# Partial sums of a second matrix product held in DRAM by adding DMAs, and a filter spectrum copied once and duplicated by DMA

## Chip, cores and metric

The kernel runs on one core of a Trainium2 chip. The metric is the device time of one execution in microseconds. The core has five engines with an in-order queue each: TensorE (PE, with its weight loads shown as PEld), VectorE (DVE), ScalarE (ACT), GpSimd (POOL) and SyncE (SP, which only issues DMAs). ACT and POOL issue DMAs too.

## The reference

All arrays are float32; B = 1, S = 2048 rows, D = 576 channels, Dff = 4608.

```python
xn = layernorm(A_q)                                   # over the channels, no scale or shift
# A: two state-space convolutions and a gate
k_shift = causal conv of A_k with A_shift_k           # 4 taps for each channel
kv = k_shift * A_v
y = irfft(rfft(pad(kv)) * rfft(pad(A_ssm_k)))[:S] + kv * A_ssm_D
# B: two matrix products
h = relu(xn @ B_w1)                                   # 2048 x 576 by 576 x 4608
out = A_q + xn * y + h @ B_w2
```

## The kernel before

**Rows and batches.** The 2048 rows are 16 tiles `t` of 128 rows, four batches `b` of four tiles. Dff is cut into 18 pairs of 256. The rows go through in two halves of two batches; each half runs over all 18 pairs, so `n` counts 36 pairs, and with two batches each there are 72 visits `(n, s)` in the main loop at the end of the program.

**Two products.** A visit does the first product for 512 rows and 256 columns of h. From the third pair on, `quad` does it with a Strassen-like scheme in four parts: sums of pieces of x and of w1 are made beforehand, and VectorE adds the results in PSUM (`psa`, L574, and `psb`, L577). Every float32 operand is split in a high part, made by ScalarE, and a low part, made by VectorE (`ll`, L532) or, for the weights, by GpSimd (`split_lo`, L424). `unit` does the second product for one tile and one half of the 576 output channels: 12 matmuls of 288 columns (two pairs; 6 where there is one) into one of three PSUM banks, and then VectorE adds the bank to the SBUF tile `acc` (L610 for batch 0, which also scales by the rows' 1/std, and L614). The `acc` tiles begin as x, loaded by `load_acc`; those of the first half are stored to `fin` in DRAM when the half is done.

**The convolution** is a generator, `conv`, with four stages: **k** (first step of the filter's transform, L656 with `prepare` L690), **x** (the four taps, L742 to L751, and the first step of the signal's transform), a middle stage **m** (second step for both, product of the spectra, first step back, L824 to L883) and **o** (last step back, gate and sum, L886 to L976). In stage m each of 32 groups makes its spectrum of the filter (`k1`, `k2`, four half copies by ScalarE for each half of the channels, L845 to L848), then that of the signal, multiplies, and goes back one group later. In stage o, `gate` multiplies by x less its mean, `add` scales by 1/std and adds to `acc`, or for the first half to `ft`, read back from `fin`, which is then stored to `out`.

**What sets the order.** `tick`, called from the matmul loops with the number of columns done, advances a clock and draws the next piece of `conv` when the clock allows. The constants `W_FK`, `W_FX`, `W_FM`, `W_FO` are the costs of a piece of each stage, `SHARE` the part of the work by whose end the convolution is to be finished; `begin_stream` turns them into a rate. `here` puts a piece of the convolution behind the latest work of the products on VectorE and ScalarE (`done`). A scheduler then fixes each engine's order. SP issues nearly all loads and stores in its order.

Of the kernel before, what the change touches and what calls it, by code (L numbers as in the profile page):

```python
# [17 lines left out]
P = 128  # L18
# [31 lines left out]
SHARE = 0.96  # L50
# [3 lines left out]
W_FK, W_FX, W_FM, W_FO = 1.73, 3.5, 1.94, 2.2  # L54
# [6 lines left out]
SUMS = {"b11": 0, "t1": 1, "t2": 2, "t3": 3, "t4": 4}  # L61
# [44 lines left out]
def h3_ffn_kernel(ctx: ExitStack, tc, x, k, v, shift_k, ssm_k, ssm_D, w1, w2, fwd, inv, mid, out):  # L106
# [23 lines left out]
    fin = dram.tile([HT // 2, P, 2, D], F32, name="fin")  # L130
# [23 lines left out]
    def load_x(t, tag, bufs, **queues):  # L154
        pair = xp.tile([P, 2, D], F32, tag=tag, name=f"acc{t}", bufs=bufs)
        move(pair, x, slice(t, t + 2), **queues)
        return pair

    def load_acc(t, **queues):
        pairs[t] = load_x(t, f"acc{t // BT % HB}", BT // 2, **queues)  # L160
        acc[t], acc[t + 1] = pairs[t][:, 0, :], pairs[t][:, 1, :]
# [120 lines left out]
    def first_xT(srcs):  # L282
# [5 lines left out]
        neg = zp.tile([P, BT], F32, tag="neg", name="neg")  # L288
        behind = None
        for t in range(BT):  # L290
            if t % 2 == 0:
                pair = row_tiles(t)
            xn = pair[:, t % 2, :]
            if t % 2 == 0:
                with tc.issue_after(behind.ins) if behind else nullcontext():
                    stats(t, srcs[t])
                    behind = centred(xn, srcs[t], t)
            else:
                nc.scalar.activation(xn, srcs[t], AF.Copy, scale=-1.0 / D,
                                     accum_out=neg[:, t:t + 1])  # L300
                done["act"] = nc.scalar.activation(xn, srcs[t], AF.Identity,
                                                   bias=neg[:, t:t + 1])
# [11 lines left out]
        with tc.issue_after(done["dve"].ins):  # L314
            for t in range(1, BT, 2):
                stats(t, srcs[t])
            inv_std(0, BT)

    def second_xT(srcs):
# [7 lines left out]
        xn = []  # L327
        for t in range(BT, HT):
            if t % 2 == 0:
                pair = row_tiles(t)  # L330
            xn.append(pair[:, t % 2, :])
            normalized(xn[-1], srcs[t], t)
# [229 lines left out]
    def quad(n, s, m):  # L562
# [11 lines left out]
        nc.vector.tensor_tensor(pa[:, other], pb[:, first], m5, OP.add)  # L574
        yield
        run_seq(pb[:, first], product(n, s, "s3", "t3"))
        nc.vector.tensor_tensor(pb[:, other], pb[:, first], m5, OP.add)  # L577
# [9 lines left out]
    work = []  # L587

    def unit(ns, s, b, i, h, last):
# [15 lines left out]
        for i, (a, m) in enumerate(seq):  # L605
            nc.tensor.matmul(ps[:, :NH], a, m, start=i == 0, stop=i == len(seq) - 1)  # L606
            if i % 6 == 5:
                tick(6 * NH)
        if b == 0:
            done["acc"] = nc.vector.scalar_tensor_tensor(  # L610
# [544 lines left out]
```

## Time and profile before

| what | value |
|---|---|
| three runs | 1133.09, 1128.83, 1132.33 us; median 1132.33 |
| the profiled execution, its own time | 1130.09 us |
| its span in the profile | 1128.1 us |
| mean granted TensorE clock | 0.98 |
| HBM read and written | 122.12 MB and 43.25 MB |

The span is from the first to the last instruction of the profile; some 2 us lie around it. All rows and windows in this document are of profiled executions, and in us from the start of the span. In the windows of the prediction the stages of the convolution lie about so: the first pairs before it 0 to 140, loads of the filter 140 to 200, stage k 200 to 312, stage x 312 to 550, the change to the second half and the start of stage m 550 to 600, stage m to 950, stage o 950 to 1092, the last units to 1128.

### The profile page before, as it was taken

To read this page: it belongs to the slowest core of one execution; us is meant where nothing else is said; L and a number is where in the kernel's file an instruction comes from. 1 tells how busy PE (TensorE), PEld (TensorE's weight loads), DVE (VectorE), ACT (ScalarE), POOL (GpSimd) and SP (SyncE) were. 2 spreads that over 40 slices of the span, in tenths; PEclk is the share of its full clock that TensorE was granted. 3 is DMA by queue.
4 is the path that set the end of the run, shared out by engine and by line. 5 is a ranking of instruction groups with operands and counts; after the bars stand their busy time and mean duration, and the time that the engine had idled before them with its cause. 6 is when DMAs were issued, how large, how long until landed. Compare 5 with 4: busy or idle time off the path is not lost.

```text
span 1128.1 us, 21092 instructions
## 1 busy us (share of the span) xinstructions
PE 1067.1 (95%) x7761; PEld 1025.5 (91%) x7761; DVE 803.6 (71%) x1309; ACT 668.3 (59%) x1454; POOL 489.6 (43%) x492
## 2 busy tenths in 40 slices
PE   8979998999988798898999999999999999999998
PEld 5779998999988788898998999999999999999897
DVE  5578733677759999888466667676576665589985
ACT  4434422798824444443368878888887887465451
POOL 3243444455435444564433344433343443545541
PEclk9998998999998999998999999999999999999999
DMA  6035598355574554453894434442334432666654
GB/s 173 25 96 189 214 147 133 114 161 165 167 200 143 159 149 136 140 166 106 300 321 129 128 108 119 121 135 87 111 113 133 119 116 93 168 176 175 206 167 105
DMA packets 139154, 166.75 MB, mean 148 GB/s; under 512 B 47566, under 2 KB 99536, under 8 KB 138541
## 3 DMA queue, kind: packets, MB, share of 16 engines
q1 hardware_dynamic: 126156, 151.24, 46.7%
q0 software_dynamic: 12576, 13.44, 5.2%
q8 instruction: 61, 1.00, 0.4%
q10 hardware_dynamic: 320, 0.74, 0.3%
q14 instruction: 41, 0.33, 0.1%
HBM read 122.12 MB, written 43.25 MB: 147 GB/s over the span
## 4 chain that ended last, share of the span: by engine, by line
PE 67%; DVE 17%; DMA 5%; SPq 4%; issue 3%; ACT 3%; POOL 1%; POOLq 0%; DVEq 0%; ACTq 0%
PE pso L606 28%; PE psb L525 18%; PE psa L525 8%; PE psf L824 6%; DVE e L745 3%; SPq L679 3%; PE psh L525 2%; DVE c L746 2%; PE psf L656 2%; DMA r<-in_w 1%; DVE xs L650 1%; DVE ll L532 1%; DVE acc L614 1%; DVE acc L610 1%; DVE c L751 1%
## 5 line engine op out<-in xcount | busy, mean ns | idle before, releaser
L606 PE MATMUL pso<-w,hh 128*128 128x288 f32 x2304 | 469.9, 298 | 11.0 <-DVE acc L610 6.9
L606 PEld LDWEIGHTS pso<-w,hh 128*128 128x128 f32 x2304 | 371.6, 190 | 20.9 <-DVE acc L610 7.8
L424 POOL TENSOR_TENSOR g<-r,g 128x512 fp32r<-128x512 f32 (+2 forms) x178 | 207.4, 1174 | 379.2 <-ACT g L453 297.4
L606 PE MATMUL pso<-w,ll 128*128 128x288 f32 x1152 | 320.8, 297 | 3.9 <-DVE ll L532 3.9
L525 PE MATMUL psb<-t,g 128*128 128x256 f32 x1632 | 248.2, 287 | 26.2 <-DVE psa L574 14.1
L525 PEld LDWEIGHTS psb<-t,g 128*128 128x128 f32 x1632 | 220.3, 191 | 33.7 <-DVE psa L574 16.7
L606 PEld LDWEIGHTS pso<-w,ll 128*128 128x128 f32 x1152 | 211.3, 190 | 6.5 <-DVE ll L532 4.8
L424 POOL TENSOR_TENSOR w<-r,w 128x576 fp32r<-128x576 f32 x72 | 114.6, 1593 | 73.1 <-ACT w L511 72.9
L478 POOL TENSOR_TENSOR r<-r 128x256 f32<-128x256 f32 x136 | 115.6, 868 | 62.2 <-DMA r<-in_w 59.8
L614 DVE TENSOR_TENSOR acc<-pso,acc 128x288 f32<-128x288 f32 x224 | 96.7, 450 | 57.7 <-PE pso L606 56.9
L525 PE MATMUL psa<-b,g 128*128 128x256 f32 x816 | 122.1, 286 | 0.0
L531 ACT ACTIVATE hh<-psa 128x512 fp32r<-128x512 f32 x68 | 40.7, 598 | 127.2 <-PE psa L525 126.8
L525 PEld LDWEIGHTS psa<-b,g 128*128 128x128 f32 x816 | 109.8, 193 | 0.2
L453 ACT ACTIVATE g<-r 128x512 fp32r<-128x512 f32 (+2 forms) x178 | 91.2, 535 | 29.3 <-POOL r L478 12.1
L532 DVE SCALAR_TENSOR_TENSOR ll<-psa,hh 128x512 fp32r<-128x512 f32 x68 | 46.7, 686 | 39.7 <-ACT hh L531 39.5
L531 ACT ACTIVATE hh<-psb 128x512 fp32r<-128x512 f32 x68 | 40.7, 598 | 49.3 <-PE psb L525 46.5
L532 DVE SCALAR_TENSOR_TENSOR ll<-psb,hh 128x512 fp32r<-128x512 f32 x68 | 46.6, 686 | 29.1 <-ACT hh L531 28.7
L650 DVE TENSOR_TENSOR ks<-kt,ks 64x288 fp32r<-64x288 f32 x64 | 54.4, 849 | 17.3 <-ACT ks L649 15.7
L525 PE MATMUL psb<-b,g 128*128 128x256 f32 x408 | 62.1, 286 | 0.0
L860 DVE TENSOR_TENSOR k<-psf,k 128x288 f32<-128x288 f32 x64 | 28.8, 454 | 46.0 <-ACT sw L859 37.9
L525 PEld LDWEIGHTS psb<-b,g 128*128 128x128 f32 x408 | 55.1, 193 | 0.0
L610 DVE SCALAR_TENSOR_TENSOR acc<-pso,rstd,acc 128x288 f32<-128x288 f32 x80 | 39.4, 511 | 19.7 <-PE pso L606 19.1
(138 smaller groups left out, 1778.7 us busy)
## 6 DMA issues: line engine op xcount, KB each, us to landing
r<-in_w SPq DMA_DIRECT2D x72, 288.0 KB, 4.0
r<-in_w SPq DMA_DIRECT2D x35, 512.0 KB, 4.1
zk<-zk SPq DMA_DIRECT2D x32, 288.0 KB, 2.7
zx<-zx SPq DMA_DIRECT2D x32, 288.0 KB, 3.5
ztk<-zk SPq DMA_DIRECT2D x32, 288.0 KB, 3.1
ztx<-zx SPq DMA_DIRECT2D x32, 288.0 KB, 2.9
zy<-vo SPq DMA_DIRECT2D x32, 288.0 KB, 3.4
zo<-zy SPq DMA_DIRECT2D x32, 288.0 KB, 3.6
```

The costliest lines, as they stand in the source:

```text
L424: return nc.gpsimd.tensor_tensor(dst, src, hi, OP.subtract)
L453: nc.scalar.activation(hi, src, AF.Copy)
L478: nc.gpsimd.tensor_tensor(dst, a, b, op)
L525: nc.tensor.matmul(ps, a, m, start=start and i == 0, stop=i == len(seq) - 1, skip_group_check=not start)
L531: done["act"] = nc.scalar.activation(hh, ps, AF.Relu)
L532: lows.append(nc.vector.scalar_tensor_tensor(ll, ps, 0.0, hh, op0=OP.max, op1=OP.subtract))
L606: nc.tensor.matmul(ps[:, :NH], a, m, start=i == 0, stop=i == len(seq) - 1)
L610: done["acc"] = nc.vector.scalar_tensor_tensor(acc[t][:, dc], ps[:, :NH], rstd[:, t:t + 1], acc[t][:, dc], op0=OP.mult, op1=OP.add)
L614: done["acc"] = nc.vector.tensor_tensor(acc[t][:, dc], ps[:, :NH], acc[t][:, dc], OP.add)
L650: nc.vector.tensor_tensor(dst[other], src[own], dst[own], OP.subtract)
L679: nc.sync.dma_start(kt[halves(h)[0], d:d + KD, :], src)
L824: nc.tensor.matmul(ps[:, :NH], a, m[:, cols], start=n == 0, stop=n == 2)
```

## The change

**Sums of the second product.** `acc` no longer holds sums. A DRAM tile `total` is filled with x by eight DRAM-to-DRAM DMAs near the start. Each `unit` copies its PSUM bank (scaled for batch 0) to one half of a small tile `g`, four of which rotate; ScalarE copies before the convolution begins and in its stages x and o, VectorE in stages k and m. After two units one DMA issued by GpSimd adds the tile to `total`. The last units of the second half load `total` back in pairs of tiles (`load_total`), add PSUM to it on VectorE, and store each unit to `out`. The tiles of x at the start are normalised in place. `fin` is gone: `ft` is read from `total`, and for the second half stage o adds its result to `total` by a DMA.

**Filter's spectrum.** ScalarE copies each half of `k1` and `k2` once; a DMA on SP duplicates it to the other 64 partitions. The filter's part of a group is done one group before the signal's, with three buffers instead of two. The minus sign moves from `k2` to `sw`.

**Stage o.** The gate's normalisation of x becomes one ScalarE pass with scale and bias (`shift` is -mean/std), and VectorE multiplies and adds without scaling.

**Order.** The costs of the four stages, `SHARE` and some buffer counts change; `tick` can draw two pieces after a part of `quad`, and one in a unit, after its first 6 matmuls.

```diff
-SHARE = 0.96
+SHARE = 0.955
-W_FK, W_FX, W_FM, W_FO = 1.73, 3.5, 1.94, 2.2
+W_FK, W_FX, W_FM, W_FO = 1.875, 4.06, 1.77, 2.1
+BY_ACT = "zxo"
+G_BUFS = 4
...
-    fin = dram.tile([HT // 2, P, 2, D], F32, name="fin")
+    total = dram.tile([NB, P, BT, D], F32, name="total")
...
+    def load_total(t, h):
+        b, i = divmod(t, BT)
+        pair = xp.tile([P, 2, NH], F32, tag="g", name=f"last{t}_{h}", bufs=G_BUFS)
+        nc.sync.dma_start(pair, total[b, :, i:i + 2, h * NH:(h + 1) * NH])
+        for n in range(2):
+            acc[t + n, h] = pair[:, n]
...
-            if i % 6 == 5:
-                tick(6 * NH)
+            if c % 6 == 5:
+                tick(6 * NH, c == 5)
+        if final:
+            if h == 0 and i % 2 == 0:
+                for m in range(2):
+                    load_total(t, m)
+            to = acc[t, h]
+            done["acc"] = nc.vector.tensor_tensor(to, ps[:, :NH], to, OP.add)
+            for u, queue in ((0, nc.sync), (1, nc.scalar if t == T - 1 else nc.sync)):
+                queue.dma_start(out[u, :, t, dc], to[halves(u)[0]])
+            return
+        if i % 2 == 0:
+            g = xp.tile([P, 2, NH], F32, tag="g", name=f"sum{ns[0]}_{t}_{h}", bufs=G_BUFS)
+            parts_[0] = g
+        to, src = parts_[0][:, i % 2], ps[:, :NH]
+        act = stage[0] in BY_ACT
         if b == 0:
-            done["acc"] = nc.vector.scalar_tensor_tensor(
-                acc[t][:, dc], ps[:, :NH], rstd[:, t:t + 1], acc[t][:, dc],
-                op0=OP.mult, op1=OP.add)
+            if act:
+                done["act"] = nc.scalar.activation(to, src, AF.Copy, scale=rstd[:, t:t + 1])
+            else:
+                done["acc"] = nc.vector.tensor_scalar(to, src, rstd[:, t:t + 1], None,
+                                                      op0=OP.mult)
+        elif act:
+            done["act"] = nc.scalar.activation(to, src, AF.Copy)
         else:
-            done["acc"] = nc.vector.tensor_tensor(acc[t][:, dc], ps[:, :NH], acc[t][:, dc],
-                                                  OP.add)
+            done["acc"] = nc.vector.tensor_copy(to, src)
+        if i % 2:
+            nc.gpsimd.dma_start(total[b, :, i - 1:i + 1, dc], parts_[0], accum_op=OP.add)
...
                         ps, cols = run(*parts["k", g], 0, h)
                         nc.scalar.activation(k1[:64, cols], ps[:64], AF.Copy)
-                        nc.scalar.activation(k1[64:, cols], ps[:64], AF.Copy)
-                        nc.scalar.activation(k2[:64, cols], ps[64:], AF.Copy, scale=-1.0)
                         nc.scalar.activation(k2[64:, cols], ps[64:], AF.Copy)
+                        if h:
+                            nc.sync.dma_start(k1[64:], k1[:64])
+                            nc.sync.dma_start(k2[:64], k2[64:])
...
-                        nc.vector.scalar_tensor_tensor(ys[i], rest[i][1], mv[:, t, 0:1], ys[i],
-                                                       op0=OP.subtract, op1=OP.mult)
+                        q = rest[i][1]
+                        nc.scalar.activation(q, q, AF.Identity, scale=rstd[:, t:t + 1],
+                                             bias=shift[:, t:t + 1])
+                        nc.vector.tensor_tensor(ys[i], ys[i], q, OP.mult)
...
                     else:
+                        nc.gpsimd.dma_start(total[t // BT, :, t % BT, :], ys[i],
+                                            accum_op=OP.add)
                         added.add(t)
...
+    for b in range(NB):
+        for u in range(U):
+            nc.sync.dma_start(total[b, halves(u)[0]], x[u, :, b * BT:(b + 1) * BT, :])
```

What this does to the order on the engines is shown at three places. The first is VectorE in stage x. Before, about the eleventh pair (`pso_6_1` is the bank of tile 6, second half; `c` and `e` are the taps):

```order
L614 TENSOR_TENSOR acc_226<-pso_4_1_4410,acc_226 128x288
L745 TENSOR_TENSOR e_3_4156<-k_3460,sk 128x576
L577 TENSOR_TENSOR psb_0_4181<-psb_0_4181,m_11_0_4195 128x256
L746 TENSOR_TENSOR c_4102<-c_4102,e_3_4156 128x576
L614 TENSOR_TENSOR acc_226<-pso_5_1_4453,acc_226 128x288
L751 TENSOR_TENSOR c_4102<-c_4102,v_4049 128x576
L745 TENSOR_TENSOR e_1_4256<-k_4046,sk 128x576
L532 SCALAR_TENSOR_TENSOR ll_0_0_4296<-psa_0_4182,hh_0_0_4295 128x512
L614 TENSOR_TENSOR acc_229<-pso_6_1_4505,acc_229 128x288
```

and VectorE in the changed kernel, one pair later in the same stage:

```order
L578 TENSOR_TENSOR psa_0_4473<-psb_0_4472,m_12_0_4486 128x256
L760 TENSOR_TENSOR c_4531<-k_4442,sk 128x576
L763 TENSOR_TENSOR e_1_4541<-k_4285,sk 128x576
L764 TENSOR_TENSOR c_4531<-c_4531,e_1_4541 128x576
L581 TENSOR_TENSOR psb_0_4472<-psb_0_4472,m_12_0_4486 128x256
L763 TENSOR_TENSOR e_2_4583<-k_4146,sk 128x576
L764 TENSOR_TENSOR c_4531<-c_4531,e_2_4583 128x576
L536 SCALAR_TENSOR_TENSOR ll_0_0_4575<-psa_0_4473,hh_0_0_4574 128x512
```

The rows that empty a PSUM bank of the second product stand no longer between the taps; they are on ScalarE.

The second place is GpSimd in stage x, with the weights of the eleventh pair (`r_11`; `g` and `w` are split weights, `wx` constants of the transform). Before:

```order
L424 TENSOR_TENSOR g_0_3818<-r_11_3639,g_0_3818 128x512
L424 TENSOR_TENSOR w_10_1_3854<-r_10_1_3565,w_10_1_3854 128x576
L424 TENSOR_TENSOR g_1_3851<-r_11_3639,g_1_3851 128x512
L424 TENSOR_TENSOR g_2_3895<-r_11_3639,g_2_3895 128x512
L424 TENSOR_TENSOR g_3_3939<-r_11_3639,g_3_3939 128x256 x2
```

and GpSimd with the same weights in the changed kernel:

```order
L428 TENSOR_TENSOR g_0_3903<-r_11_3719,g_0_3903 128x512
L428 TENSOR_TENSOR w_10_1_3940<-r_10_1_3646,w_10_1_3940 128x576
L656 DMA wx_4081<-in_fwd 128x256
L639 DMA total<-sum_0_0_3922 128x2x288
L428 TENSOR_TENSOR g_1_3937<-r_11_3719,g_1_3937 128x512
L639 DMA total<-sum_2_0_4001 128x2x288
L428 TENSOR_TENSOR g_2_3982<-r_11_3719,g_2_3982 128x512
```

The adding DMAs, each of which waits for a copy on ScalarE, now stand between the splits of the weights.

The third place is SP at the end of the program. Before, only the outputs of the last tiles stand there:

```order
L150 DMA out<-acc_6989 64x1152 x2
L150 DMA out<-acc_6992 64x1152 x2
L150 DMA out<-acc_6740 64x1152 x2
L150 DMA out<-acc_6743 64x576 x2
L618 DMA out<-acc_6743 64x288 x2
```

and SP at the end of the changed kernel (`last_0` and `last_1` are the two halves of the channels; the last two of them are tiles 14 and 15):

```order
L621 DMA out<-last_0_14399 64x288 x2
L621 DMA out<-last_1_14401 64x288 x2
L621 DMA out<-last_0_14399 64x288 x2
L621 DMA out<-last_1_14401 64x288 x2
L167 DMA last_0_14443<-total 128x2x288
L167 DMA last_1_14445<-total 128x2x288
L621 DMA out<-last_0_14443 64x288 x2
```

The loads of the sums of tiles 14 and 15 stand behind the outputs of tiles 12 and 13. At the other end of SP's queue, the eight DMAs that fill `total` stand behind the loads of x for the second batch and ahead of the second pair's weights.

More of the change, by code (lines that the diff above doesn't have):

```diff
@@ L326, in second_xT @@
             inv_std(BT, BT)
[L327 to L332, printed above, removed]
+        xn = [srcs[t] for t in range(BT, HT)]
+        for i, row in enumerate(xn):
+            normalized(row, row, BT + i)
         for c in range(5):
@@ L664, in here @@
             yield
+    stage = ["z"]
+    shift = const.tile([P, T], F32, name="shift")
     def conv():
+        stage[0] = "k"
         with tc.tile_pool(name="fk", bufs=2) as fp:
@@ L1120, in h3_ffn_kernel @@
             phase([n], s, b, True)
-        if half == 1 and m == 0:
-            base = HT + (1 - second) * BT
-            for t in range(base, base + BT, 2):
-                load_acc(t)
     while work:
```

152 lines of the change are left out of this document (78 added, 74 removed).

## The prediction

> **What bounds the kernel now.** I read the page first, then the table of windows with one row per stage, then TensorE's waits inside the one stage that stands out, then VectorE's groups there.
>
> ```profile
> PE 1067.1 (95%) x7761; PEld 1025.5 (91%) x7761; DVE 803.6 (71%) x1309; ACT 668.3 (59%) x1454; POOL 489.6 (43%) x492
> ```
>
> TensorE is busy 95% of the span, so at first sight nothing but fewer matmuls could help, and the change removes none. The table by stage says more (columns: window, its length, then busy time and instruction count of PE, PEld, DVE, ACT, POOL, then clock, DMA share, GB/s).
>
> ```profile
> core 0: us, PE busy (x) PEld busy (x) DVE busy (x) ACT busy (x) POOL busy (x), PEclk, DMA share, GB/s
> 0.00:140.00 140.00, 125.13 (x779) 108.51 (x779) 97.58 (x201) 57.78 (x118) 51.55 (x54) 0.96 0.46 139
> 140.00:200.00 60.00, 55.20 (x399) 54.03 (x400) 19.66 (x37) 15.05 (x31) 25.90 (x29) 0.94 1.02 135
> 200.00:312.00 112.00, 110.05 (x830) 107.27 (x829) 84.06 (x125) 96.53 (x187) 58.12 (x69) 1.00 0.52 156
> 312.00:550.00 238.00, 211.10 (x1492) 201.06 (x1491) 202.67 (x278) 94.75 (x202) 114.57 (x112) 0.96 0.53 152
> 550.00:600.00 50.00, 50.00 (x384) 49.37 (x383) 29.29 (x54) 29.44 (x66) 20.47 (x21) 1.00 0.96 320
> 600.00:950.00 350.00, 347.64 (x2627) 341.77 (x2626) 234.75 (x385) 291.05 (x671) 142.08 (x126) 1.00 0.38 115
> 950.00:1092.00 142.00, 138.43 (x1046) 135.25 (x1045) 112.80 (x189) 74.94 (x162) 72.30 (x77) 1.00 0.63 179
> 1092.00:1128.00 36.00, 29.56 (x217) 28.27 (x215) 22.83 (x43) 8.76 (x20) 4.61 (x7) 0.96 0.40 104
> ```
>
> I take 550 to 600 as TensorE undisturbed: 384 matmuls in 50 us, 7.68 per us. From 140 us on, all stages hold the same mixture of 256- and 288-column matmuls, so a window's count over 7.68 is the time its work needs. Stage k (200 to 312) needs 108.1 of 112, **stage x (312 to 550) 194.3 of 238, a loss of 43.7 us**, 600 to 950 needs 342.1 of 350, stage o (950 to 1092) 136.2 of 142. In stage x VectorE was busy 202.67 us: more than the 194.3 TensorE needs. Elsewhere VectorE's share of the needed time is 0.78 (k), 0.69 (600 to 950), 0.83 (o). So stage x is bound by VectorE; TensorE bounds the rest but for the two ends. What TensorE waited for in stage x agrees (columns: waiter, releaser, us in total, times, longest):
>
> ```profile
> PE psb L525 <- DVE psa L574: 12.6, 6, 4.5
> PE pso L606 <- DVE acc L610: 5.2, 2, 4.1
> PE pso L606 <- DVE ll L532: 3.4, 3, 1.3
> PE psf L656 <- DVE xs L650: 2.0, 3, 0.8
> ```
>
> Every releaser is VectorE.
>
> **The change, part by part.**
>
> *Stage x: the adds leave VectorE.* Groups of VectorE in 312 to 550:
>
> ```profile
> L610 DVE SCALAR_TENSOR_TENSOR acc<-pso,rstd,acc 128x288 f32<-128x288 f32 x32 | 15.7, 510 | 5.4 <-PE pso L606 5.1
> L614 DVE TENSOR_TENSOR acc<-pso,acc 128x288 f32<-128x288 f32 x25 | 10.8, 446 | 1.9 <-PE pso L606 1.9
> L532 DVE SCALAR_TENSOR_TENSOR ll<-psa,hh 128x512 fp32r<-128x512 f32 x14 | 9.6, 685 | 5.0 <-ACT hh L531 5.0
> L532 DVE SCALAR_TENSOR_TENSOR ll<-psb,hh 128x512 fp32r<-128x512 f32 x14 | 9.6, 685 | 7.3 <-ACT hh L531 7.3
> L577 DVE TENSOR_TENSOR psb<-psb,m 128x256 f32<-128x256 f32 x15 | 6.4, 427 | 3.5 <-PE psb L525 3.5
> L574 DVE TENSOR_TENSOR psa<-psb,m 128x256 f32<-128x256 f32 x15 | 6.3, 420 | 2.2 <-PE psb L525 2.2
> ```
>
> 57 adds go, 15.7 + 10.8 = 26.5 us. The last four rows are the feed-forward work that stays, 31.9 us. Stage x is also spread over more of that work: its cost number goes from 3.5 to 4.06, and by the formula of `begin_stream` one unit of cost now takes 0.986 of the columns, so the feed-forward part grows by 1.144. Of the 194.3 us the stage's own 128 matmuls take 128/7.68 = 16.7; the other 177.6 become 203.2. New need: 220 us of TensorE against 202.67 - 26.5 + 0.144 x 31.9 = 181 us of VectorE, a share of 0.82, as in stage o now. Stage o lost 5.8 of 136.2 (4.3%), stage k at 0.78 lost 3.9 of 108.1 (3.6%); 4% of 220 is 9 us. One wait stays, at the stage's start:
>
> ```profile
> 317.73 8.26 DMA k-1_3456<-in_k
> 326.08 1.06 DVE L745 TENSOR_TENSOR e<-k-1_3456,sk 128x576 f32<-128x576 f32 x1 [5.66 <-DMA k-1_3456<-in_k]
> ```
>
> VectorE is in order and stands 5.66 us before its first tap; the new order keeps this tap behind the same load, with a first-product addition behind it. I leave 4 us for it. Loss after: 13; gain 43.7 - 13 = **30.7 us**.
>
> Part of that gain is clock. The row of stage x grants 0.96, 9.5 us of 238, where 200 to 312 and 550 to 1092 have 1.00, and its two longest waits are 4.5 and 4.1 us. [...]
>
> *What the ScalarE copies, POOL issues and DMAs cost.* Nearest rows:
>
> ```profile
> L657 ACT ACTIVATE zx<-psf 128x288 f32<-128x288 f32 x64 | 23.4, 410 | 34.9 <-issue 21.9 <-PE psf L656 10.8 <-ACT zx L657 1.2
> L643 POOL DMA_DIRECT2D wk<-in_fwd x32 | 17.4, 545 | 17.6 <-PE psf L656 17.5
> L435 POOL DMA_DIRECT2D r<-in_w x1 | 0.9, 902 | 0.4 <-issue 0.4
> q1 hardware_dynamic: 126156, 151.24, 46.7%
> q0 software_dynamic: 12576, 13.44, 5.2%
> zk<-zk SPq DMA_DIRECT2D x32, 288.0 KB, 2.7
> r<-in_w POOLq DMA_DIRECT2D x1, 256.0 KB, 8.0
> ```
>
> 144 copies go to ScalarE at 0.41 us each, 59 us; in stage x some 60 of them bring it from 94.75 of 238 to about 120 of 233: hidden. The other 144 stay on VectorE (k and the middle stage) as plain copies; no such copy is shown, bounds are 0.38 below and the add's 0.45 above, and I count no gain, since TensorE hardly waits there. POOL issues 152 more DMAs: 0.55 (128 rows) to 0.90 us (512 rows), for 256 rows 0.65, so 99 us on an engine idle 638 us. Each waits on POOL for its copy, with weight splits queued behind it; those are made a visit (about 15 us) ahead. An adding DMA is in no row. Below: 256 packets at the mean of q1 (0.467 x 1128 x 16 / 126156 = 67 ns) are 1.07 us of all 16 engines; above, four times that. I take twice, 2.1 us, because the target is read and written. One starts every 7.5 us, 0.28 of the DMA, beside 0.53 in stage x: hidden. Landing 2.7 to 8.0 us; four `g` tiles cover three intervals, 22 us.
>
> *140 to 200* has the DMA at 1.02 already. Eight adding DMAs are 17 us more there, 0 to 17 on the path; weights wait behind the filter's loads on SP. I take **+2**.
>
> *Stage o.* The adds and the `acc` additions leave VectorE:
>
> ```profile
> L614 DVE TENSOR_TENSOR acc<-pso,acc 128x288 f32<-128x288 f32 x40 | 17.3, 449 | 15.4 <-PE pso L606 15.2
> L935 DVE SCALAR_TENSOR_TENSOR acc<-y,rstd,acc 128x576 f32<-128x576 f32 x8 | 8.5, 1067 | 0.1
> ```
>
> 112.80 - 17.3 - 8.5 = 87 us for 130 us of TensorE (the stage shrinks by 0.948), 0.67: the loss of 600 to 950 (2.3%), 3 us instead of 5.8, **-3**. The gate's extra ScalarE pass is hidden by ScalarE's 67 idle us.
>
> *Middle stage.* 128 half copies leave ScalarE, and each group's k half runs a group ahead; 64 duplicating DMAs wait on SP for ScalarE, with the z loads behind them. A group lasts about 350/30 = 11.7 us, over the 2.7 to 8.0 us above: hidden. Of the 7.9 us lost in 600 to 950 I take **-2.5**, at the start, where groups ran without a lead. If the DMA landed late, each group would lose the excess.
>
> *Start.* Eight DRAM copies of 590 KB stand on SP ahead of the second weights:
>
> ```profile
> 17.73 0.37 SPq L435 DMA_DIRECT2D r<-in_w  x1
> 42.88 1.55 ACT L453 ACTIVATE g<-r 128x512 fp32r<-128x512 f32 x4
> ```
>
> These weights were asked for at 17.73 and split at 42.88. 4.7 MB at the 320 GB/s of 550 to 600 take 15 us, at half that rate 29; begun near 13 us, they end at 28 to 42, and the weights land 4 us later: 0 to 3 us late, 1 taken. VectorE's adds there (70% busy) move to ScalarE, worth 3 of the 14.9 us idle. Together **-2** (-8 to +3).
>
> *End.* The last loads of sums stand behind the outputs of tile 13:
>
> ```profile
> 1115.30 7.47 PE pso L606 x56
> 1122.79 0.46 DVE acc L614
> ```
>
> A unit of 6 takes 0.8 us. Three PSUM banks let TensorE run 2.4 us past tile 13 while its add, issue and landing take some 0.5 + 1.5 + 4: **+4** (0 to 7).
>
> **Sum**, on the profiled execution's 1130.09 us: -30.7 - 3 - 2.5 - 2 + 2 + 4 = -32.2, so **1098 us**. The runs' median is 2.2 above that execution, inside the range.
>
> **Rivals.** (a) *VectorE still binds stage x by order*: the taps stay about 1 us each in front of the psa and psb additions, and half the loss stays, 22 us instead of 13, with nothing won at start, middle or end: about 1115. For it, psa L574 is the largest releaser; against it, stage o runs at 0.83 with few losses. (b) *The DMA becomes the bound, slower than before*: with an adding DMA at four times a plain one, 4.3 us, stage x needs 0.53 x 238 + 29 x 4.3 = 251 us, 31 over 220, and 140 to 200 needs 61 + 8 x 4.3 = 95, 35 over: 1098 + 66 = 1164. It decides in stage x from (220 - 126)/29 = 3.2 us per adding DMA; for it speaks the 1.02 row, against it the 0.38 in the middle. (c) *POOL's order*: copies hold POOL, weight splits come late, TensorE waits in x and o for weights, and the gain is returned: 1130. For it, POOL waits for others most of its time; against it, 43% busy and a visit's lead. (d) *It does more*: the start's and k's losses go too, 1075.
>
> **Chances.** Forecast (1080 to 1112) 0.60; (a) 0.17; (c) 0.08; (b) 0.11; (d) 0.04. The predicted time is the likeliest's, 1098. The range, 1078 to 1136, takes in (a), (c) and the bounds of start and end. A measurement tells 0.5% (5.7 us) from no change: faster 0.80, same 0.08, slower 0.12.
>
> **What would show it.** In the new windows, stage x should hold a count near 7.35 per us with VectorE near 0.8 and clock 1.00; a DMA share near 1 there shows (b); waits of TensorE for weights show (c); TensorE waiting for psa with taps in front shows (a). A gap of 3 us or more before the last unit shows the end's term. I am wrong if stage x's 43.7 us were not VectorE's, or if an adding DMA holds the engines over 3 us.

## Result: 2.9% slower, and the profile after

| | before | changed |
|---|---|---|
| median of the runs (4 each) | 1131.56 us | 1164.40 us (1162.21 to 1164.93) |
| ratio, 95% interval | 1 | 1.0289 (1.0265 to 1.0314) |
| profiled execution, its span | 1130.09, 1128.1 us | 1164.32, 1162.5 us |
| mean granted clock | 0.98 | 0.967 |

One of the four executions of e12 (below), the profiled one, took 3590.82 us; the time given for e12 is the median of the other three.

The page of the changed kernel: engines, DMA queues, the adding DMA's issue and its landing:

```profile
PE 1069.3 (92%) x7761; PEld 1029.7 (89%) x7761; DVE 780.0 (67%) x1160; ACT 682.6 (59%) x1486; POOL 659.5 (57%) x644
q1 hardware_dynamic: 134476, 163.04, 48.5%
q0 software_dynamic: 52896, 58.28, 32.0%
L639 POOL DMA_DIRECT2D total<-sum x144 | 186.4, 1313 | 106.3 <-DVE sum L637 26.9
total<-sum POOLq DMA_DIRECT2D x144, 288.0 KB, 6.1
r<-in_w SPq DMA_DIRECT2D x35, 512.0 KB, 6.3
```

The record of an adding DMA on POOL lasts 1.31 us, and the DMA lands in 6.1. POOL's busy time grew by 170 us. The windows of the changed kernel, cut at its own stages (start, loads of the filter, k, x, change of half, m, o, end; columns as in the prediction):

```profile
0.00:150.00 150.00, 131.37 (x820) 115.55 (x821) 85.83 (x179) 69.02 (x148) 70.58 (x73) 0.94 0.75 196
150.00:212.00 62.00, 48.90 (x357) 47.55 (x356) 16.20 (x32) 13.84 (x29) 29.93 (x29) 0.89 1.08 150
212.00:325.00 113.00, 104.91 (x773) 100.27 (x773) 83.68 (x114) 94.95 (x185) 74.16 (x83) 1.00 0.78 192
325.00:590.00 265.00, 235.22 (x1682) 227.09 (x1680) 214.29 (x230) 126.36 (x285) 162.95 (x155) 0.95 0.80 194
590.00:617.00 27.00, 27.00 (x209) 26.65 (x208) 10.66 (x21) 11.58 (x27) 20.97 (x22) 1.00 1.06 244
617.00:968.00 351.00, 350.42 (x2672) 346.02 (x2672) 251.36 (x403) 258.41 (x580) 194.67 (x173) 1.00 0.77 185
968.00:1130.00 162.00, 148.78 (x1101) 144.63 (x1101) 106.84 (x161) 105.65 (x231) 102.79 (x108) 0.97 0.91 221
1130.00:1162.00 32.00, 22.69 (x164) 21.92 (x162) 11.09 (x23) 2.81 (x6) 3.41 (x5) 0.89 0.53 139
```

With the prediction's measure, need = matmuls / 7.68 per us, the loss of each stage comes out so (the end taken to 1162.5; the start, which holds other shapes, by its count at the rate of before: 820/779 x 140 = 147.4 of 150):

| stage | lost before | lost after | difference | forecast |
|---|---|---|---|---|
| start | | | +2.6 | -2 |
| loads of the filter | 8.0 | 15.5 | +7.5 | +2 |
| k | 3.9 | 12.3 | +8.4 | 0 |
| x | 43.7 | 46.0 | +2.3 | -30.7 |
| change of half and m | 7.9 | 2.9 | -5.0 | -2.5 |
| o | 5.8 | 18.6 | +12.8 | -3 |
| end | 7.7 | 11.1 | +3.4 | +4 |

**Stage x.** 57 additions left VectorE and yet it was busy 214.29 us of a need of 1682/7.68 = 219.0. Where they went is in VectorE's groups of stage x, before (312 to 550):

```profile
L745 DVE TENSOR_TENSOR e<-k,sk 128x576 f32<-128x576 f32 x42 | 42.6, 1014 | 0.5
L746 DVE TENSOR_TENSOR c<-c,e 128x576 f32<-128x576 f32 x48 | 42.1, 878 | 0.4
L650 DVE TENSOR_TENSOR xs<-c,xs 64x576 fp32r<-64x576 f32 x32 | 31.5, 983 | 1.2 <-ACT xs L649 0.2
L751 DVE TENSOR_TENSOR c<-c,v 128x576 f32<-128x576 f32 x16 | 18.8, 1175 | 0.3
L742 DVE TENSOR_TENSOR c<-k,sk 128x576 f32<-128x576 f32 x16 | 14.6, 911 | 0.0
```

and of the changed kernel (325 to 590):

```profile
L764 DVE TENSOR_TENSOR c<-c,e 128x576 f32<-128x576 f32 x48 | 57.0, 1187 | 1.0
L763 DVE TENSOR_TENSOR e<-k,sk 128x576 f32<-128x576 f32 x42 | 50.9, 1211 | 0.5
L663 DVE TENSOR_TENSOR xs<-c,xs 64x576 fp32r<-64x576 f32 x32 | 29.5, 922 | 8.5 <-ACT xs L662 7.7
L769 DVE TENSOR_TENSOR c<-c,v 128x576 f32<-128x576 f32 x16 | 20.6, 1285 | 0.3
L760 DVE TENSOR_TENSOR c<-k,sk 128x576 f32<-128x576 f32 x16 | 16.7, 1043 | 1.9 <-DMA k<-in_k 1.8
```

The same 154 instructions on the same shapes take 174.7 us instead of 149.6: 25.1 of the 26.5 us that the additions freed. Most of that is not the adding DMAs': in e1 (below), which has the rest of the change without them, the same 154 take 164.5 us, 15 of the 25.1. Its two largest groups (302 to 546):

```profile
L762 DVE TENSOR_TENSOR c<-c,e 128x576 f32<-128x576 f32 x48 | 54.4, 1134 | 0.9
L761 DVE TENSOR_TENSOR e<-k,sk 128x576 f32<-128x576 f32 x42 | 44.3, 1054 | 0.5
```

What TensorE waited for in stage x of the changed kernel (waiter, releaser, us in total, times, longest; the three largest):

```profile
PE psb L529 <- DVE ll L536: 10.2, 4, 4.1
PE psb L529 <- DVE psa L578: 8.0, 2, 7.7
PE psb L529 <- DVE psb L581: 4.5, 2, 3.2
```

The other two are for ScalarE's `psa` (3.7) and VectorE's `xs` (2.9); none is for a weight. The longest, 7.7 us, stands behind the stage's first tap, before which VectorE stood for a load:

```profile
340.37 0.76 DVE L763 TENSOR_TENSOR e<-k-1_3555,sk 128x576 f32<-128x576 f32 x1 [8.66 <-DMA k-1_3555<-in_k]
```

Other waits stand behind long taps: one of 2.78 us that ends at 468.14 behind a tap of 4.63 us; VectorE's timeline of the changed kernel around that tap (start, duration):

```profile
461.07 0.43 DVE L581 TENSOR_TENSOR psb<-psb,m 128x256 f32<-128x256 f32 x1
461.41 1.40 DVE L763 TENSOR_TENSOR e<-k,sk 128x576 f32<-128x576 f32 x1
462.85 4.63 DVE L764 TENSOR_TENSOR c<-c,e 128x576 f32<-128x576 f32 x1
```

and POOL's at the same time:

```profile
462.15 1.21 POOL L639 DMA_DIRECT2D total<-sum  x1
462.92 1.04 POOL L656 DMA_DIRECT2D wx<-in_fwd  x1
463.53 1.75 POOL L428 TENSOR_TENSOR g<-r,g 128x512 fp32r<-128x512 f32 x1
464.79 1.84 POOL L428 TENSOR_TENSOR w<-r,w 128x576 fp32r<-128x576 f32 x1
466.14 1.64 POOL L639 DMA_DIRECT2D total<-sum  x1
```

I sorted all VectorE operations with two SBUF inputs and over 0.6 us by what POOL did meanwhile. In the changed kernel the 163 beside an idle POOL took 0.73 us on average, 76 beside DMA issues alone 0.73, 124 beside POOL's tensor operations 1.11, 107 beside tensor operations and issues 1.60. (Before: 212 at 0.73, 19 at 0.72, 188 at 1.20, 30 at 1.10.) So issues by themselves drew out nothing on VectorE here: 0.73 us beside them and 0.73 beside an idle POOL. That splits crowded between issues delay more than others is suggested and not shown: an operation that has been drawn out meets more of POOL's records for that very reason, and in e1, sorted alike, some 40 operations beside both, without any adding DMA, also took about 1.6 us. Why these operations took 1.11 to 1.60 us beside POOL's tensor operations and 0.73 without them was not shown. The one of 4.63 us (462.85 to 467.48) overlaps all five records of POOL shown above, two of them splits of 1.75 and 1.84 us.

**Stage o.** TensorE's largest wait in stage o (waiter, releaser, us in total, times, longest):

```profile
PE pso L611 <- POOL w L428: 9.7, 2, 9.3
```

and POOL's timeline of the changed kernel there (in brackets the idle time before and its releaser):

```profile
1052.05 0.89 POOL L975 DMA_DIRECT2D total<-y  x1 [4.00 <-DMA total<-sum]
...
1064.95 1.19 POOL L975 DMA_DIRECT2D total<-y  x1
1073.93 1.20 POOL L639 DMA_DIRECT2D total<-sum  x1 [7.79 <-DMA total<-y]
```

An adding DMA to rows of `total` stood on POOL until one before it to the same rows had landed, here 4.00 and 7.79 us. The weight split `w` stands behind it; TensorE's wait ends at 1078.43.

**Loads of the filter.** TensorE waited 12.5 us for ACT `g`, and that for POOL's sums of w1. POOL's timeline:

```profile
200.66 2.09 POOL L482 TENSOR_TENSOR r<-r 128x256 f32<-128x256 f32 x3 [14.26 <-DMA r<-in_w]
```

and SP's, which issued that load behind seven of the filter's (before, at 176.75):

```profile
175.74 18.23 SPq L696 DMA_DIRECT2D kt<-in_ssm_k  x7
194.07 2.10 SPq L439 DMA_DIRECT2D r<-in_w  x1
```

### The profile page after: what moved, and what is told of

It reads as the page before. It is cut to its first block, busy times and chain, and to the rows that moved or that the text cites. A ratio compares the mean times of both kernels' runs of the same rounds, so it can differ in the third digit from the quotient of the medians.

```text
span 1162.5 us, 21633 instructions
## 1 busy us (share of the span) xinstructions
PE 1069.3 (92%) x7761; PEld 1029.7 (89%) x7761; DVE 780.0 (67%) x1160; ACT 682.6 (59%) x1486; POOL 659.5 (57%) x644
## 5 line engine op out<-in xcount | busy, mean ns | idle before, releaser
L428 POOL TENSOR_TENSOR g<-r,g 128x512 fp32r<-128x512 f32 (+2 forms) x178 | 231.3, 1355 | 172.5 <-ACT g L457 136.8
L639 POOL DMA_DIRECT2D total<-sum x144 | 186.4, 1313 | 106.3 <-DVE sum L637 26.9
L482 POOL TENSOR_TENSOR r<-r 128x256 f32<-128x256 f32 x136 | 121.8, 919 | 106.9 <-DMA r<-in_w 105.0
L428 POOL TENSOR_TENSOR w<-r,w 128x576 fp32r<-128x576 f32 x72 | 121.4, 1687 | 32.6 <-ACT w L515 32.3
L637 DVE COPY sum<-pso 128x288 f32<-128x288 f32 x117 | 51.0, 450 | 34.2 <-PE pso L611 33.9
L663 DVE TENSOR_TENSOR ks<-kt,ks 64x288 fp32r<-64x288 f32 x64 | 58.5, 913 | 17.6 <-ACT ks L662 16.2
L578 DVE TENSOR_TENSOR psa<-psb,m 128x256 f32<-128x256 f32 x68 | 29.1, 428 | 59.4 <-PE psb L529 43.1
L764 DVE TENSOR_TENSOR c<-c,e 128x576 f32<-128x576 f32 x48 | 57.0, 1187 | 1.0
```

Of the source, the lines that this page charges most:

```text
L428: return nc.gpsimd.tensor_tensor(dst, src, hi, OP.subtract)
L482: nc.gpsimd.tensor_tensor(dst, a, b, op)
L578: done["acc"] = nc.vector.tensor_tensor(pa[:, other], pb[:, first], m5, OP.add)
L637: done["acc"] = nc.vector.tensor_copy(to, src)
L639: nc.gpsimd.dma_start(total[b, :, i - 1:i + 1, dc], parts_[0], accum_op=OP.add)
L663: nc.vector.tensor_tensor(dst[other], src[own], dst[own], OP.subtract)
```

## The experiments

Theory P: POOL's time is what the adding DMAs cost. Theory T, later A: it is their traffic, or something that only adding packets do. Theory O: it is the new order. Ratios are to the kernel before, with 95% intervals.

### What the adding DMAs cost in all: e1 to e4

e1 leaves the units' adding DMAs out, but keeps the copies to `g`. e2 puts two plain stores on SP in their place, e3 one plain store on GpSimd, e4 one adding DMA for four units:

```diff
-            nc.gpsimd.dma_start(total[b, :, i - 1:i + 1, dc], parts_[0], accum_op=OP.add)
+            for to in (total, total2):                                              # e2
+                nc.sync.dma_start(to[b, :, i - 1:i + 1, dc], parts_[0])
...
+            nc.gpsimd.dma_start(total[b, :, i - 1:i + 1, dc], parts_[0])            # e3
...
+        if i % 2 and h:                                  # e4: g holds both halves of D
+            nc.gpsimd.dma_start(total[b, :, i - 1:i + 1, :], parts_[t - 1], accum_op=OP.add)
```

> The changed kernel without the 144 adding DMAs of the units' sums; the copies to g stay (left out of the output: every sum but the last pair's). Theory P (GpSimd: 144 issues at 1.31 us hold POOL, weight splits come late, and VectorE's two-input operations stand beside more POOL work) and theory T (DMA traffic: the adding packets take 32% of the 16 engines, loads land late) both expect the added losses of stages k, x, o, of the filter's loads and of the start to go: 1095 to 1115 us. Theory O (the new order and ScalarE's copies, not the DMAs) expects 1150 or more.

> The changed kernel with each adding DMA replaced by two plain stores of the same tile, issued by SP, to two DRAM tensors (the sums are not formed). The DMA engines carry 512 packets of 1152 bytes where the adding DMA carried 256 of twice the duration, so the DMA's load is about kept, and POOL is relieved of 186 us. Theory P expects most of the loss gone: 1100 to 1120 us, POOL busy back near 470 us, VectorE's two-input operations in stage x back to some 36 us of waiting instead of 61. Theory T expects 1150 to 1170.

> The changed kernel with accum_op left out: GpSimd issues 144 plain stores of 256 rows (the sums are not formed). Theory T expects q0's packets to go from 129 ns to some 60 ns, its share from 32% to some 17%, and half of the loss or more gone: 1130 or less. Theory P goes by the issue: if a plain issue of 256 rows still takes 1.1 us or more, 1150 to 1165; if it takes 0.65, about 1130 too, and then only e2 decides.

> The same sums with one adding DMA for four units instead of two: a tile g holds two row tiles with both halves of the channels, so that a DMA writes 128 rows of 4608 bytes instead of 256 of 1152; 72 issues instead of 144, three buffers. The bytes stay. Stage o's 8 adding DMAs of 128 rows took 0.99 us to issue (0.86 at least), so POOL gives back some 189 - 72 x 0.9 = 124 us. Theory P expects about two thirds of the loss gone, 1120 to 1135; theory T expects 1150 to 1165 unless long packets are cheaper per byte than 0.098 ns, then in proportion.

| | us | ratio | POOL busy | DMA share q1 + q0 |
|---|---|---|---|---|
| changed | 1164.4 | 1.0289 (1.0265 to 1.0314) | 659.5 | 80.5% |
| e1 | 1104.5 | 0.9763 (0.9734 to 0.9791) | 496.4 | 58.5% |
| e2 | 1112.2 | 0.9835 (0.9799 to 0.9872) | 495.9 | 79.2% |
| e3 | 1125.9 | 0.9953 (0.9931 to 0.9975) | 598.2 | 67.4% |
| e4 | 1137.1 | 1.0061 (1.0034 to 1.0089) | 550.5 | 76.0% |

Theory O falls: without the DMAs the rest of the change is 2.4% faster than before. The DMA load of e2 costs 8 of the 60 us between e1 and the changed kernel; it is 79.2% of 1110.9 less 58.5% of 1102.3 us, 235 us of all 16 engines, where the adding DMAs put 32.0% of 1162.5 less 6.8% of 1102.3, 297 us. So theory T fails on e2, which it put at 1150 to 1170. e3 missed as a test: its stores went out as 64 packets of 4608 bytes each, and an issue took 0.735 us. e4 saves 109 us of POOL and 27 us of time, but at less POOL time it is slower than e3: against theory P alone. The adding DMA's own weight is as forecast: 297/144 = 2.06 us.

### POOL's time and DMA load apart: e5, e6, e9, e10, e17

Tiny plain DMAs of the same tile stand in for the time that the adding DMA holds POOL; e6, e10 and e17 have e2's stores by SP besides.

```diff
+            for m in range(2):                                                      # e5, e6
+                nc.gpsimd.dma_start(scrap[m, :, :, None], parts_[0][:, :, m:m + 1])
...
+            for m in range(2):                                                      # e9, e10
+                nc.gpsimd.dma_start(scrap[b, :, i - 1:i, h * NH + 32 * m:h * NH + 32 * m + 16],
+                                    parts_[0][:, m:m + 1, :16])
...
+            for m in range(2):                                                      # e17
+                nc.gpsimd.dma_start(
+                    scrap[b, :, i - 1:i + 1, h * NH + 32 * m:h * NH + 32 * m + 16],
+                    parts_[0][:, :, 32 * m:32 * m + 16])
```

> The changed kernel with each adding DMA replaced by two plain DMAs of GpSimd that store 256 single values of the same tile (the sums are not formed): POOL waits for the same copies and is held by two issues of some 0.7 us, 1.4 us together, about the adding DMA's 1.31, but next to no bytes move. It stands against the 1104.5 us without any of these DMAs and the changed kernel's 1164. Theory P (POOL's time alone, holding back splits behind it): 1145 to 1160 us. Theory A (the adding packets themselves: 112 ns each, loads landing at 5.3 instead of 3.9 us): 1105 to 1125.

> Both stand-ins at once: the two tiny DMAs of GpSimd for POOL's time, and two plain stores by SP for the DMA's load (the sums are not formed). If the changed kernel's loss is POOL's time plus DMA load and nothing that only adding packets do, this gives the changed kernel's time: 1155 to 1170 us. If the adding packets have an effect of their own, it stays at 1115 to 1140.

e5 took 1885 us and e6 2086, and neither tests what it was made for: all stores went to one address range, and they stood on POOL for stores before them to land. POOL's waits of e5 (us in total, times, longest) price that wait:

```profile
POOL scrap L641 <- DMA scrap<-sum: 676.6, 128, 11.2
```

> As the earlier run with tiny DMAs, whose stores all went to one small DRAM tile so that each waited for the one before to land; now each pair of units has its own addresses. In place of the adding DMA GpSimd issues two plain DMAs of 128 rows of 64 bytes (the sums are not formed): two issues at 0.55 us, 1.1 us together against the adding DMA's 1.31, with hardly any bytes. Theory P (POOL's time): 1140 to 1155 us. Theory A (the adding packets and their landing): 1105 to 1125.

> The same two tiny DMAs on GpSimd, and besides them the two plain stores by SP that gave 1112 us alone (the sums are not formed). POOL's time plus DMA load without any adding packet. If the two together are the changed kernel's loss: 1148 to 1165. If adding packets have an effect of their own: 1115 to 1135.

> The run with two tiny DMAs of GpSimd and two plain stores by SP (1138 us), but each tiny DMA with 256 rows instead of 128: its issue should go from 0.56 to some 0.73 us, 1.45 us for a pair of units instead of 1.13, so that the adding DMA's 1.31 lies between. No adding packets (the sums are not formed). If the rest of the changed kernel's loss is POOL's time too, at a rate that grows as POOL fills: 1158 to 1175 us. If it is something of the adding packets: 1140 to 1152.

| ratio to before | no stores | two stores by SP |
|---|---|---|
| POOL free | 0.9763 (e1) | 0.9835 (e2) |
| two issues, 1.13 us | 0.9873 (0.9852 to 0.9895) (e9, 1116.8 us) | 1.0056 (1.0034 to 1.0077) (e10, 1138.4 us) |
| two issues, 1.49 us | | 1.0186 (1.0148 to 1.0224) (e17, 1149.1 us) |

By itself the DMA load costs 0.7%, POOL's time 1.1%; together 2.9%, which is 1.1% more than their sum (give or take 0.6%, by the four intervals), and 4.2% with the longer issues. The adding DMAs cost 5.3%.

How much of the 5.3% this explains depends on how well POOL's time is matched, and there the records leave room, since those of POOL overlap. By POOL's busy time (over e1: 163 us more in the changed kernel, 141 in e10, 206 in e17) the changed kernel lies a third of the way from e10 to e17, which gives 1.010: 3.4 of the 5.3%. By starts it is less: where another instruction of POOL follows at once, it starts 0.86 us after an adding DMA (mean of 77), while e10's two issues together hold back what follows by 1.13 us and e17's two by 1.46. Between e2, at nothing, and e10 that gives 1.000: 2.4 of the 5.3%. e17 holds POOL longer than the changed kernel by both measures, so its 4.2% is an upper bound. By these two measures a little under half to two thirds of the loss come without one adding packet, from two things that cost more together than their sum. Neither theory had that: e9 fell in A's range, e10 between the two, and e17 in A's range again. The rest, 21 to 32 us (12 at the least, 1.0289 less 1.0186), comes only with adding packets. Some of it may be load, of which e10 and e17 add less to the engines (257 and 264 us over e1, against 291). How the two delays come to add was not shown. A chain that they share, by the code, is that of a pair's weights: a load, sums on POOL, a split on ScalarE, a split on POOL, and the buffer's next load; but in stage x of the changed kernel TensorE waited for no weight. Stage x in e1, e2, e9, e10 and e17 (windows, one row each):

```profile
302.00:546.00 244.00, 231.20 (x1707) 224.91 (x1706) 197.65 (x230) 126.18 (x287) 133.81 (x125) 0.98 0.58 175
```
```profile
309.00:553.00 244.00, 231.48 (x1712) 224.42 (x1711) 199.71 (x231) 126.76 (x287) 131.29 (x125) 0.99 0.81 254
```
```profile
312.00:555.00 243.00, 218.70 (x1581) 208.91 (x1580) 204.99 (x225) 121.60 (x274) 150.69 (x177) 0.98 0.58 174
```
```profile
324.00:574.00 250.00, 219.83 (x1574) 210.38 (x1574) 202.04 (x225) 122.31 (x276) 150.15 (x181) 0.97 0.77 235
```
```profile
322.00:582.00 260.00, 234.83 (x1657) 224.98 (x1657) 203.63 (x231) 128.60 (x292) 167.70 (x186) 0.95 0.80 245
```

Losses by the same measure: 21.7, 21.1, 37.1, 45.1 and 44.2 us, against 46.0 in the changed kernel (one profile each). Here load alone costs nothing, POOL's issues 15 us, both 23, nearly all of the 24 us between e1 and the changed kernel, without an adding packet. VectorE's share of the need goes from 0.89 (e1) to 1.00 (e9), more because e9's window holds less work of TensorE (205.9 us of need, e1's 222.3) than because VectorE does more (205.0 us, 197.7). The length of VectorE's instructions does not follow these losses: the same 154 instructions take 164.5 us in e1, 164.5 in e2, 170.9 in e9 (153 of them), 168.1 in e10, 166.4 in e17. So it is not drawn-out instructions that make e10 and e17 lose more than e9; what does stays open. The wait at the stage's start is a part: TensorE's wait there was 3.0 us in e1, 4.0 in e2, 3.6 in e9, 6.2 in e10, 6.5 in e17 and 7.7 in the changed kernel.

### Less work on POOL: e7, e11, e12

e7 gives GpSimd's sums of pieces of w1 (L482) to ScalarE as copies; e11 (changed kernel) and e12 (before) leave them out and split the pieces themselves.

```diff
-        nc.gpsimd.tensor_tensor(dst, a, b, op)
+        with at_turn(n):                                                            # e7
+            nc.scalar.activation(dst, a, AF.Copy)
...
-        nc.gpsimd.tensor_tensor(dst, a, b, op)                                      # e11, e12
...
-            split_into(n, two[0], two[1], r1[:, 5:9, right])
+            split_into(n, two[0], two[1], r1[:, 0:4, right])
```

> The changed kernel with all 144 adding DMAs, but the 136 sums of pieces of w1 (0.92 us each on GpSimd, 125 us together) replaced by ScalarE copies of their first operand (left out: those sums, so the first product is not the reference's). POOL falls to about 535 us, near the kernel before. Theory P expects most of the loss back: 1115 to 1135 us. Theory A expects 1150 or more.

> The changed kernel with all adding DMAs, but without GpSimd's 136 sums of pieces of w1 (the splits read the pieces themselves; left out: those sums, so the first product is not the reference's). No other engine takes the work over, as ScalarE did in the run at 1185 us, where ScalarE then stood 106 us before loads of w1. POOL falls by 125 us to some 535. Theory P: 1120 to 1135 us. Theory A: 1150 or more.

> The control for the run before it: the kernel before without the 136 sums of pieces of w1 (left out: those sums). POOL falls from 490 to some 370 us, with it some of the 36 us that VectorE's two-input operations lose in stage x: 1115 to 1128. What the changed kernel gains more than this by the same edit is what POOL's time costs it beyond the kernel before.

e7 took 1185.3 us, ratio 1.0484 (1.0443 to 1.0526), with POOL at 543.7: ScalarE then stood 106 us before loads of w1, with the copies that TensorE needs behind it. In e7's groups:

```profile
L483 ACT ACTIVATE r<-r 128x256 f32<-128x256 f32 x136 | 54.7, 413 | 107.5 <-DMA r<-in_w 105.6
```

e11 took 1145.1 us, 1.0110 (1.0073 to 1.0147), e12 1116.7 us, 0.9861 (0.9840 to 0.9882). e11 fell between the two theories' ranges. The same relief gives the changed kernel 1.7% and the kernel before 1.4%, which the intervals do not tell apart. So this pair shows that POOL's time is dear in both kernels, not that it is dearer in the changed one; taking 116 us of it from the changed one brings back 19 of the 60 us.

### The order among adding DMAs: e13, e14

e13 stores stage o's results to a tile of their own; e14 issues each adding DMA one pair of units later.

```diff
-                        nc.gpsimd.dma_start(total[t // BT, :, t % BT, :], ys[i],    # e13
-                                            accum_op=OP.add)
+                        nc.gpsimd.dma_start(apart[t // BT, :, t % BT, :], ys[i])
...
-            nc.gpsimd.dma_start(total[b, :, i - 1:i + 1, dc], parts_[0], accum_op=OP.add)
+            flush()                                                                 # e14
+            held.append((total[b, :, i - 1:i + 1, dc], parts_[0]))
```

> The changed kernel, but stage o's eight results of the second half are stored to a DRAM tile of their own instead of being added to total (left out: those rows' convolution part of the output). All 144 adding DMAs of sums stay. In the changed kernel's stage o GpSimd stood 1.3, 4.0 and 7.8 us because an adding DMA to rows of total waits for the landing of the one before it on the same rows, and TensorE then stood 9.6 us for a weight split. If this order of adding DMAs is what adding packets cost beyond POOL's time and DMA load in stage o: its loss falls from 18.3 to 4 to 8 us, 1150 to 1156 us in all. If stage o is late for loads and POOL's time alone: 1160 to 1166.

> The changed kernel with each adding DMA issued by GpSimd one pair of units later (five tiles g instead of four), so that its copies are long done. POOL's 144 issues, their 1.31 us and the DMA load stay; what goes is POOL standing before them (some 80 us of waits for copies in the profile) with weight splits behind. If that standing holds the splits back: 1140 to 1152. If it is the time of the issues and the DMA load: 1158 to 1170.

e13 took 1161.4 us, 1.0242 (1.0189 to 1.0295). Its stage o:

```profile
970.00:1126.00 156.00, 149.25 (x1116) 145.92 (x1115) 113.52 (x165) 106.65 (x232) 100.39 (x109) 0.99 0.92 230
```

Loss 156 - 1116/7.68 = 10.7 us instead of 18.6, and the 9.6 us gap is gone, so the order of adding DMAs made that gap; but the whole gained only 3 us, and the interval of its ratio holds the changed kernel's. e14 took 1168.6 us, 1.0318 (1.0280 to 1.0356). It tests nothing: POOL still waited 64 us for copies ahead of its adding DMAs (25.8, 20.5 and 17.5 us) as in the changed kernel (26.9, 21.2 and 17.0), so what was to go did not go.

### Stage x without adding DMAs: e8, e15, e16, e18

The filter's part of the change, put into the kernel before (`vo` and `yl` with one buffer for room), with sums in SBUF as before (e8; stage m is then as in the diff of the change); then with other costs of stages x and m.

```diff
-W_FK, W_FX, W_FM, W_FO = 1.73, 3.5, 1.94, 2.2
+W_FK, W_FX, W_FM, W_FO = 1.73, 4.06, 1.77, 2.2   # e15
+W_FK, W_FX, W_FM, W_FO = 1.73, 4.6, 1.6, 2.2     # e16
+W_FK, W_FX, W_FM, W_FO = 1.73, 5.0, 1.47, 2.2    # e18
```

> The kernel before with the filter's part of the change alone (copied once, duplicated by DMA, a group ahead; sums stay in SBUF, old costs). For room, vo and yl have one buffer instead of two. The changed kernel's middle stage lost 1.6 us where the one before lost 6.7, so 3 to 6 us should be won: 1125 to 1128 us against some 1131. If the single buffers cost more than that, 1131 to 1140.

> The kernel before with the filter's part alone (1124.9 us), and the changed kernel's costs for stages x and m (4.06 and 1.77 instead of 3.5 and 1.94): stage x is spread over more of the products' work, 275 us instead of 238. Sums stay in SBUF by VectorE. If stage x's 45 us of loss come of VectorE having too much work in it (217 of 238 us): VectorE would stand at about 227 of 275, where the run without adding DMAs lost 21 at 207 of 244, so 1108 to 1116. If they come of the taps standing in front of the products' additions whatever the share: 1122 to 1127.

> The same with costs of 4.6 and 1.6: stage x over some 310 us with VectorE at 237 of them, stage m over some 290 us, where ScalarE would be at 252 and VectorE at 245. VectorE's share theory: stage x loses 12 to 18 instead of 45, stage m gives 5 to 12 back: 1103 to 1116. By order alone: 1125 or more.

> The kernel before with the filter's part and costs of 5.0 and 1.47 for stages x and m, one step beyond the run at 1110.4 us (stage x 32 us lost with VectorE at 239 of 270, stage m 0.7). VectorE's share theory: stage x over some 290 us loses 20 to 27, stage m over some 310 us 1 to 6: 1100 to 1110. If stage m now runs into ScalarE (279 of 335 before, some 0.87 then): 1110 to 1120.

| | us | ratio | stage x: length, VectorE / need, lost | stage m lost |
|---|---|---|---|---|
| e8 | 1124.9 | 0.9939 (0.9914 to 0.9964) | 238, 1.06, 45.7 | 2.1 |
| e15 | 1122.2 | 0.9917 (0.9899 to 0.9934) | 263, 0.98, 45.0 | 2.9 |
| e16 | 1110.4 | 0.9806 (0.9787 to 0.9824) | 270, 0.94, 32.6 | 2.2 |
| e18 | 1112.1 | 0.9837 (0.9795 to 0.9878) | 288, 0.90, 32.4 | 2.2 |

Rows of e16, stages x and m:

```profile
310.00:580.00 270.00, 249.95 (x1823) 240.25 (x1822) 222.33 (x316) 107.83 (x229) 138.06 (x132) 0.98 0.61 180
610.00:945.00 335.00, 335.00 (x2556) 331.13 (x2555) 248.85 (x394) 254.01 (x575) 129.89 (x115) 1.00 0.52 149
```

**e16 beats both kernels**, by 1.9% and 4.7% (0.9806/1.0289). The copied and duplicated spectrum is worth 0.6% alone; it leaves stage m with slack, and a shorter m lets stage x be spread. The new costs were not run without the spectrum's part, so that they need its slack is argued and not shown. Neither reading of stage x came out whole: e15 lost as much as e8 at a lower share (as by order), e16 lost 13 us less (as by share), e18 no less than e16 at 0.90. What holds the last 32 us was not settled.

## Why the prediction was wrong

1098 us were forecast (1078 to 1136), 1164.4 measured. Point by point:

- **Stage x, -30.7, came to +2.3.** The need was right (220; 219.0 measured). The step that failed is "202.67 - 26.5 + 0.144 x 31.9 = 181 us of VectorE": it took over unchanged the durations of the taps and of the stage's other operations with two SBUF inputs. They went with what POOL did: such an operation beside POOL's tensor operations took 1.1 to 1.6 us and alone 0.73. VectorE came to 214, its 154 instructions to 174.7 us where they had been 149.6, and 15 of these 25 us are there without the adding DMAs (e1). e1's VectorE is at 197.65 of 222.3 and loses 21.7 us, so that even without them only 22 of the 30.7 were to be had: a share of 0.89 lost 10%, where 4% was taken over from stages k and o. The other 24 us come with POOL's issues and DMA load (e9, e10), and the length of those instructions does not account for them. One term of the sum was too small besides: the wait at the stage's start, put at 4 us, was 7.7. The clock, to which part of the gain was put down, was 0.95 where it had been 0.96 (0.98 in e1, 0.95 in e17); what lowers it was not shown. (The sign of 7.35 per us does not follow from the prediction's own sum, 220 of 233 us, which gives 7.25; measured were 1682/265 = 6.35.)
- **The adding DMAs' issues, "99 us on an engine idle 638 us", hidden.** Mis-sized: the record is 1.31 us and not 0.65, 186 us in all, though what follows on POOL starts 0.86 us later. And not hidden: the idle share of POOL was taken for cover, but issues by themselves cost 1.1% (e9 against e1), and 2.9% together with a DMA load that alone costs 0.7% (e2, e10).
- **The DMA's load** was right: 2.1 us taken, 2.06 measured; landing of 6.1 inside 2.7 to 8.0. "Hidden" was right for it alone (e2: 8 us in all, none in stage x).
- **140 to 200, +2 (0 to 17)**: +7.5, inside the bounds. e10 waits 11.5 us there without adding packets (the changed kernel 12.5), e9 4.7, so it too is load and POOL together.
- **Stage o, -3, came to +12.8.** Not priced: an adding DMA waited on POOL for the landing of one before it on the same rows (4.00 and 7.79 us), with weight splits behind (e13: 8 us of it, one profile each). POOL's time with load is in it too: e17, by the same measure, loses 146 - 1025/7.68 = 12.5 us there, e10 4.3.
- **Middle, -2.5**: -5.0, the mechanism right. e8 shows it alone.
- **Start, -2**: +2.6, inside -8 to +3. **End, +4**: +3.4, with the gap before the last unit (5.5 us), and the same in e1.
- **Stage k, 0**: +8.4, not settled. TensorE's largest wait there is for the constants `wk` that GpSimd loads, 3.6 us in six waits. e1 and e2 lose 13.4 and 16.9 us in it (742 matmuls in 110 us, 738 in 113), e9 and e10, with POOL busier, 4.4 and 6.8 (865 in 117, 877 in 121), so the adding DMAs are not needed for it.
- **The rivals.** (a), half of stage x's loss kept because VectorE still binds it, put 22 us on that stage, which is what e1 loses without the adding DMAs (21.7); the changed kernel then loses as much again. (b) gave 1164 by a DMA that binds at 4.3 us an adding DMA; it is 2.06, so its number is an accident. (c), POOL's order, named the right engine, and TensorE did wait for weights at the filter's loads and in stage o, but not in stage x; at 1130 and with 8% it was priced by POOL's 43%.

The 21 to 32 us that come only with adding packets (12 at the least) have no cause shown; the order of adding DMAs to the same rows may be 3 of them (e13).

## What to carry to other kernels

Price work that moves to GpSimd's queue by what stands behind it and beside it: the splits that follow an issue, and the VectorE operations with two SBUF inputs that meet those splits, whose duration was no constant here (0.73 us alone, 1.1 to 1.6 beside them). An engine idle 57% of the time is no cover by that alone when its work is a link of a chain that also waits for loads: test the two delays together, since their sum was not additive here. And when a part of a change makes slack in one stage, move that slack to the stage that lacks it before paying for more.

## What the runs showed of the hardware

- An adding DMA of 256 rows of 1152 bytes had a record of 1.31 us on GpSimd in the changed kernel, where a plain one of the same tile had 0.735 (e3). The records overlap with the next: an instruction that followed at once started 0.86 us after the adding one (mean of 77) and 0.75 after the plain one (mean of 62). Its packets took the engines about two and a half times as long as those of a plain store (297 us of all engines for 144, against 235 us for the 288 plain stores of e2: 2.06 and 0.82 us each).
- A VectorE operation of 0.73 us with two SBUF inputs lasted 4.63 us beside a run of GpSimd operations, and 0.73 us beside issues of DMAs alone (mean of 76), both in the changed kernel.
- Where GpSimd's DMAs went to the same addresses, they waited for DMAs before them to land: 676.6 us in 128 waits in e5.
